# Own PSUM tiles for weight products and transposes, and value turns one to a step, in an attention and max-out kernel

## Chip, cores and metric

One core of one Trainium2 chip runs the kernel. The metric is device time in microseconds (us), lower is better.

## The reference, cut to what matters

```python
# attention over 4 x 8 heads, sequence 768, head size 64; keys and values are first
# mixed over 8 blocks of 96 by a matrix P made from sort_net (softmax and column sums, 5 rounds)
k_sorted = einsum('bhij,bhjcd->bhicd', P, k_blocks)
v_sorted = einsum('bhij,bhjcd->bhicd', P, v_blocks)
attn = softmax(q_block @ k_sorted_block.T / 8)          # each block of 96 on its own
x = (attn @ v_sorted_block)                             # -> 3072 tokens x 512
# max-out layer
h1, h2 = x @ w1, x @ w2                                 # 512 -> 1024
return maximum(h1, h2) @ w_out                          # 1024 -> 512
```

The kernel uses max(h1, h2) = max(h1 - h2, 0) + h2. It makes g = relu(x (W1 - W2)), and for the h2 part it multiplies W2 with Wout once (the "W2 Wout product", wc), so that the output is g Wout + x wc.

## The kernel before

Batch 0 runs its attention, and the weights are prepared beside it. Later batches' attention is woven between the matmuls of the layer. Everything that TensorE (PE) writes lands in PSUM, and here in one pool of four PSUM tiles, each of two banks:

```python
psum = ctx.enter_context(tc.tile_pool(name="psum", bufs=4, space=bass.MemoryType.PSUM))
def ps_f32(name):
    return psum.tile([128, 1024], FP32, tag="ps", name=name)
def ps_bf16(name):
    return psum.tile([128, 2048], BF16, tag="ps", name=name)
```

A new tile takes a place that an earlier tile has left; its first matmul waits until the earlier tile has been evicted (copied out or read for the last time) by ScalarE (ACT, "A") or VectorE (DVE, "D"). To multiply W2 with Wout, W2 is transposed by PE in two lots of 16 blocks; the second lot is evicted half by ACT, half by DVE:

```python
    def w2_transposes(t, eng):
        ps = ps_bf16("tw_ps")
        for n in range(16):
            fb, dmt = t * 4 + n // 4, n % 4
            nc.tensor.matmul(
                ps[:, n * 128 : (n + 1) * 128],
                w2_sb[:, dmt, fb * 128 : (fb + 1) * 128],
                ident,
                is_transpose=True,
                start=True,
                stop=True,
            )
        def out():
            w = 2048 // len(eng)
            for n, e in enumerate(eng):
                evac(
                    w2T[:, t * 4 : t * 4 + 4, :].rearrange("p f d -> p (f d)")[
                        :, n * w : (n + 1) * w
                    ],
                    ps[:, n * w : (n + 1) * w],
                    w,
                    two_x=True,
                    eng=e,
                )

        return out

    wc_ps = {}

    def w_product(dmt, eng=None):
        m = dmt % 2
        if m == 0:
            wc_ps[0] = ps_f32("wc_ps")
        for fb in range(NFB):
            nc.tensor.matmul(
                wc_ps[0][:, m * 512 : (m + 1) * 512],
                w2T[:, fb, dmt * 128 : (dmt + 1) * 128],
                wo_sb[:, fb, :],
                start=(fb == 0),
                stop=(fb == NFB - 1),
            )
        if m == 1:
            evac(wc[:, dmt - 1 : dmt + 1, :].rearrange("p t n -> p (t n)"), wc_ps[0], 1024, eng=eng)
```

So two products share one tile, which is held from the first product to the end of the second. The order of the steps that the change touches (cut; the comments are added here):

```python
tail = {
    ...
    3: [
        VA[6],                                  # values 6: attention output, step 6 of steps 0 to 7
        VA[7],
        lambda: w2_transposes(1, "AD")(),
        lambda: x_transposes(0, 2, "A"),
        lambda: [turn(second, c) for c in (0, 12, 24)],
    ],
    ...
# batch 0, weaving in batch 1's attention: value turns (a DVE copy that reorders values for batch 2)
VA[1:6] = [(lambda f=f, g=g: (f(), g())) for f, g in zip(VA[1:6], tns)]
TR[0:2] = [(lambda f=f, g=g: (f(), g())) for f, g in zip(TR[0:2], tns[5:])]
SC[7:] = [lambda f=SC[7], g=tns[7]: (f(), g())]
```

`TR[0]` runs in the same step as `VA[1]`, so two turns stand in a row behind values 1. A values step ends with a reciprocal and a multiply (x) on DVE, which free its PSUM tile.

The softmax here doesn't subtract the row's maximum and nothing guards it: scores larger than these inputs give would overflow.

## Time and profile before

| | before |
|---|---|
| median of 3 runs | 171.54 us (171.15 to 171.66) |
| span of the profiled run | 169.6 us |
| PE busy | 162.3 us, 96% |
| DVE, ACT busy | 54%, 47% |
| share of PE in the chain that ended last | 87% |

A line of the timeline has the start, the length, engine and source line, the operation, output <- inputs with shapes, how many instructions were merged, and in brackets the idle time before it and what ended that. A line of the chain has start, length, and engine, tile and source line. The chain is found from the last instruction backwards: at each step what released it, or the instruction before it on its engine. A matmul's end is modelled by the profiler; its start is recorded. PEld is PE's weight load. The tiles in these lines: o_ps is the attention output of a values step, s_ps the scores, tq_ps query transposes, tx_ps x transposes, v_ps the mixing ("sort") of the values, tw_ps and w2T the transposed W2, wc_ps the W2 Wout products, h_ps and out_ps the layer's two matmuls.

### The profile page before, as it was taken

How to read it: one execution, taken by the hardware profiler on the slowest of the kernel's cores; microseconds unless marked ns; L12 is line 12 of the kernel's file. 1: busy time of each engine (PE TensorE's matmuls, PEld its weight loads, DVE VectorE, ACT ScalarE, POOL GpSimd, SP SyncE). 2: the span in 40 equal slices, each digit the busy share in tenths (PEclk: the TensorE clock that was granted, in tenths of full speed). 3: DMA queues.
4: the chain of work that ended last, by engine and by line, in shares of the span. 5: the costliest groups of instructions: out<-in, count | busy, mean ns of one | idle time of the engine just before them, and what ended most of it. 6: DMA issues, size and time to landing. Idle time of an engine off the chain costs nothing.

```text
span 169.6 us, 4551 instructions
## 1 busy us (share of the span) xinstructions
PE 162.3 (96%) x2015; PEld 97.0 (57%) x2015; DVE 91.8 (54%) x198; ACT 80.4 (47%) x98; POOL 25.3 (15%) x40
## 2 busy tenths in 40 slices
PE   7799999999999999999999999999999999999991
PEld 7638766736666554457665545566554546654461
DVE  4979677689245399847674448074552422330040
ACT  3598975756855554046774350446505404312000
POOL 7944372243300000000510000000000000000000
PEclk9999999999999999999999999999999999999999
DMA  3999999999999652994199349930025173000342
GB/s 47 201 206 207 199 207 206 209 202 206 215 220 198 106 170 52 140 238 151 10 199 169 92 126 215 194 120 6 0 50 150 34 203 128 0 0 0 124 157 94
DMA packets 29811, 23.11 MB, mean 136 GB/s; under 512 B 16672, under 2 KB 24736, under 8 KB 29792
## 3 DMA queue, kind: packets, MB, share of 16 engines
q0 software_dynamic: 10304, 12.58, 43.7%
q1 hardware_dynamic: 19200, 10.04, 23.9%
q8 instruction: 16, 0.26, 0.6%
q10 hardware_dynamic: 288, 0.20, 0.4%
q14 instruction: 3, 0.02, 0.0%
HBM read 25.17 MB, written 6.29 MB: 186 GB/s over the span
## 4 chain that ended last, share of the span: by engine, by line
PE 87%; DVE 6%; ACT 3%; DMA 1%; issue 1%
PE out_ps L608 37%; PE h_ps L581 26%; PE o_ps L471 5%; PE k_ps L377 4%; PE s_ps L444 4%; PE wc_ps L559 3%; PE v_ps L398 2%; PE v_ps L419 1%; PE tw_ps L529 1%; PE tq_ps L347 1%; DMA p_sb<-in_sort_net_dram 1%; PE tq_ps L352 1%; DVE colsum L226 1%; PE o_ps L81 1%; PE tx_ps L509 1%
## 5 line engine op out<-in xcount | busy, mean ns | idle before, releaser
L608 PE MATMUL out_ps<-wo_sb,g 128*128 128x512 bf16 (+2 forms) x208 | 48.3, 363 | 0.0
L581 PE MATMUL h_ps<-xT,w_sb 128*128 128x384 bf16 x256 | 44.8, 326 | 0.2 <-ACT g L595 0.2
L581 PEld LDWEIGHTS <-w_sb 128*128 128x128 bf16 x256 | 24.0, 98 | 15.7 <-issue 0.2
L452 ACT ACTIVATE e<-s_ps 96x768 bf16<-96x768 f32 x32 | 24.2, 804 | 16.1 <-PE s_ps L444 15.9
L608 PEld LDWEIGHTS <-g 128*128 128x128 bf16 x208 | 17.5, 97 | 15.3
L595 ACT ACTIVATE g<-h_ps 128x768 bf16<-128x768 f32 x21 | 16.9, 810 | 18.0 <-PE h_ps L581 18.0
L608 PE MATMUL out_ps<-wc,xT 128*128 128x512 bf16 (+2 forms) x104 | 25.0, 362 | 0.0
L103 ACT COPY o<-out_ps 128x1024 f32<-128x1024 f32 x9 | 9.1, 1012 | 30.0 <-PE out_ps L608 25.7
L597 DVE TENSOR_SCALAR g<-h_ps 128x768 bf16<-128x768 f32 x11 | 10.5, 955 | 22.5 <-PE h_ps L581 22.5
L488 DVE TENSOR_TENSOR x<-o_ps,rs 96x512 bf16<-96x512 f32 x32 | 22.0, 687 | 1.1
L482 DVE RECIPROCAL rs<-o_ps 96x8 f32<-96x8 f32 x32 | 6.4, 199 | 20.5 <-PE o_ps L471 20.4
L608 PEld LDWEIGHTS <-xT 128*128 128x128 bf16 x104 | 9.9, 97 | 11.0
L209 DVE COPY v_dc<-v_raw 64x768 bf16<-64x768 bf16 (+2 forms) x18 | 15.4, 897 | 0.1
L471 PEld LDWEIGHTS <-e 96*128 96x128 bf16 x256 | 11.6, 97 | 6.7 <-DVE x L488 0.5
L471 PE MATMUL o_ps<-v_sb,e 96*128 96x65 bf16 x256 | 12.9, 193 | 0.1
L105 DVE CAST v_sb<-v_ps 96x1024 bf16<-96x1024 f32 x7 | 8.5, 1214 | 5.6 <-PE v_ps L398 5.2
L103 ACT CAST v_sb<-v_ps 96x1024 bf16<-96x1024 f32 x9 | 8.9, 1014 | 1.6 <-PE v_ps L419 1.0
L444 PEld LDWEIGHTS <-kT 64*128 64x128 bf16 x256 | 6.0, 94 | 5.4 <-issue 4.6
L444 PE MATMUL s_ps<-qT,kT 64*128 64x96 bf16 x256 | 8.6, 204 | 0.1
L103 ACT CAST kT<-k_ps 128x1024 bf16<-128x1024 f32 x8 | 7.7, 1021 | 1.1 <-PE k_ps L377 1.1
L105 DVE COPY o<-out_ps 128x1024 f32<-128x1024 f32 x2 | 2.4, 1224 | 10.6 <-PE out_ps L608 9.5
L81 PEld LDWEIGHTS <-fill 128*128 128x128 bf16 x109 | 6.9, 120 | 2.2 <-DVE fill L72 1.2
(76 smaller groups left out, 138.4 us busy)
## 6 DMA issues: line engine op xcount, KB each, us to landing
out_dram<-o SPq DMA_DIRECT2D x11, 512.0 KB, 3.1
k_raw<-in_k_dram POOLq DMA_DIRECT2D x12, 256.0 KB, 10.3
q_raw<-in_q_dram POOLq DMA_DIRECT2D x4, 768.0 KB, 12.6
v_raw<-in_v_dram POOLq DMA_DIRECT2D x6, 384.0 KB, 13.8
w_sb<-in_moe_w_dram POOLq DMA_DIRECT2D x3, 512.0 KB, 15.9
wo_sb<-in_moe_w_out_dram POOLq DMA_DIRECT2D x2, 512.0 KB, 18.8
v_raw<-in_v_dram POOLq DMA_DIRECT2D x3, 256.0 KB, 4.9
w_sb<-in_moe_w_dram POOLq DMA_DIRECT2D x2, 256.0 KB, 14.1
```

The costliest lines, as they stand in the source:

```text
L81: nc.tensor.matmul(ps[:, 0:w], w0, fill[:, 0:w], start=True, stop=True)
L103: nc.scalar.copy(out=out_ap, in_=in_ap)
L105: nc.vector.tensor_copy(out=out_ap, in_=in_ap)
L209: nc.vector.tensor_copy(out=dst, in_=src)
L444: nc.tensor.matmul(ps[:, h2 * 512 + ii * 128 : h2 * 512 + ii * 128 + BLK], kT[b][rows, (hp * 8 + i) * BLK : (hp * 8 + i) * BLK + 128], rhs ...
L452: nc.scalar.activation(out=e[:, 0 : 8 * BLK].rearrange("p (t c r) -> p t c r", t=8, r=R), in_=ps[0:BLK].rearrange("p (t f) -> p t f", t=8) ...
L471: nc.tensor.matmul(ps[:, h2 * 512 + ii * 65 : h2 * 512 + (ii + 1) * 65], e[:, (h2 * 4 + ii) * BLK : (h2 * 4 + ii) * BLK + 128], v_sb[:, m0 ...
L488: nc.vector.tensor_tensor(out=x, in0=ov[:, :, :, 0:D], in1=rs.to_broadcast([BLK, 2, 4, D]), op=ALU.mult,)
L581: nc.tensor.matmul(h_ps[t][:, m * 512 : m * 512 + TCH], w1_sb[:, hp, fb * 128 : (fb + 1) * 128], xT[:, b % 2, ch, hp % 2, hp // 2, :], sta ...
L595: nc.scalar.activation(out=g, in_=src, func=AF.Relu)
L597: nc.vector.tensor_scalar(out=g, in0=src, scalar1=0.0, scalar2=None, op0=ALU.max)
L608: nc.tensor.matmul(dst, g_tiles[b, ch, m // 2][:, m % 2, off : off + 128] if m < NFB else xT[:, b % 2, ch, hp % 2, hp // 2, off : off + 12 ...
```

## The change

The intent: no tile of products is held over other work, each half of the second transposes is in its own tile so that neither evicting engine waits for the other, the transposes come one step sooner so that their eviction lies beside the last values, and none of the eight turns for batch 2 stands directly behind another on DVE.

```diff
--- before.py
+++ after.py
@@ -523,48 +523,47 @@
     wc = big.tile([128, HP, DMODEL], BF16, tag="wc", name="wc")
 
     def w2_transposes(t, eng):
-        ps = ps_bf16("tw_ps")
-        for n in range(16):
-            fb, dmt = t * 4 + n // 4, n % 4
-            nc.tensor.matmul(
-                ps[:, n * 128 : (n + 1) * 128],
-                w2_sb[:, dmt, fb * 128 : (fb + 1) * 128],
-                ident,
-                is_transpose=True,
-                start=True,
-                stop=True,
-            )
+
+        w = 16 // len(eng)
+        outs = []
+        for p, e in enumerate(eng):
+            ps = ps_bf16("tw_ps")
+            for n in range(w):
+                fb, dmt = t * 4 + (p * w + n) // 4, n % 4
+                nc.tensor.matmul(
+                    ps[:, n * 128 : (n + 1) * 128],
+                    w2_sb[:, dmt, fb * 128 : (fb + 1) * 128],
+                    ident,
+                    is_transpose=True,
+                    start=True,
+                    stop=True,
+                )
+            outs.append((ps, p, e))
+
         def out():
-            w = 2048 // len(eng)
-            for n, e in enumerate(eng):
+            for ps, p, e in outs:
+                fb = t * 4 + p * w // 4
                 evac(
-                    w2T[:, t * 4 : t * 4 + 4, :].rearrange("p f d -> p (f d)")[
-                        :, n * w : (n + 1) * w
-                    ],
-                    ps[:, n * w : (n + 1) * w],
-                    w,
+                    w2T[:, fb : fb + w // 4, :].rearrange("p f d -> p (f d)"),
+                    ps[:, 0 : w * 128],
+                    w * 128,
                     two_x=True,
                     eng=e,
                 )
 
         return out
 
-    wc_ps = {}
-
     def w_product(dmt, eng=None):
-        m = dmt % 2
-        if m == 0:
-            wc_ps[0] = ps_f32("wc_ps")
+        ps = ps_f32("wc_ps")
         for fb in range(NFB):
             nc.tensor.matmul(
-                wc_ps[0][:, m * 512 : (m + 1) * 512],
+                ps[:, 0:512],
                 w2T[:, fb, dmt * 128 : (dmt + 1) * 128],
                 wo_sb[:, fb, :],
                 start=(fb == 0),
                 stop=(fb == NFB - 1),
             )
-        if m == 1:
-            evac(wc[:, dmt - 1 : dmt + 1, :].rearrange("p t n -> p (t n)"), wc_ps[0], 1024, eng=eng)
+        evac(wc[:, dmt, :], ps[:, 0:512], 512, eng=eng)
 
 
     g_tiles = {}
@@ -719,8 +718,8 @@
         2: [SC[6], SC[7], VA[5]],
         3: [
             VA[6],
+            lambda: w2_transposes(1, "AD")(),
             VA[7],
-            lambda: w2_transposes(1, "AD")(),
             lambda: x_transposes(0, 2, "A"),
             lambda: [turn(second, c) for c in (0, 12, 24)],
         ],
@@ -789,9 +788,8 @@
                 tail[9][2:2] = ks
                 vs = [lambda t=t: sort_v(1, t) for t in range(4)]
                 tns = [lambda c=c: turn(both, c) for c in range(0, BLK, 12)]
-                VA[1:6] = [(lambda f=f, g=g: (f(), g())) for f, g in zip(VA[1:6], tns)]
-                TR[0:2] = [(lambda f=f, g=g: (f(), g())) for f, g in zip(TR[0:2], tns[5:])]
-                SC[7:] = [lambda f=SC[7], g=tns[7]: (f(), g())]
+                for step, n in [((VA, 0), 0), ((VA, 1), 1), ((VA, 2), 2), ((VA, 4), 3), ((TR, 1), 4), ((VA, 5), 5), ((SC, 7), 6), ((VA, 6), 7)]:
+                    step[0][step[1]] = lambda f=step[0][step[1]], g=tns[n]: (f(), g())
                 steps = group(*vs[:3]) + qs[:1] + group(*SC[0:2], vs[3]) + qs[1:] + VA[:1]
                 steps += group(*SC[2:5]) + VA[1:2]
             elif b == 1:
```

## The prediction

> **What bounds the kernel now.** I read the page first: the busy shares, then the chain of work that ended last.
>
> ```profile
> PE 162.3 (96%) x2015; PEld 97.0 (57%) x2015; DVE 91.8 (54%) x198; ACT 80.4 (47%) x98; POOL 25.3 (15%) x40
> ...
> PE 87%; DVE 6%; ACT 3%; DMA 1%; issue 1%
> ```
>
> TensorE (PE) is busy 96% of a 169.6 us span and has 87% of the chain; VectorE (DVE) and ScalarE (ACT) are half idle. The clock row of the page is nine tenths or more in all 40 slices. So a change that only gives DVE or ACT less to do moves nothing. It has to remove time in which PE streams nothing. Where is such time in the part that the change touches? The chain of waits between 30 and 54 us, in order of time (start, length, what), shows each place where the chain leaves PE:
>
> ```profile
> 32.69 0.91 PE tw_ps L529 x16
> 33.60 0.02 issue
> 33.62 1.02 ACT w2T L103
> 34.64 0.02 issue
> 34.66 0.70 DVE w2T L105
> 35.37 0.05 issue
> 35.41 0.60 PE wc_ps L559 x2
> ...
> 47.60 1.02 ACT v_sb L103
> 48.62 0.04 issue
> 48.66 0.83 PE tq_ps L347 x12
> ...
> 51.25 1.02 ACT wc L103
> 52.27 0.04 issue
> 52.32 0.83 PE tq_ps L347 x12
> ```
>
> There are three. First, the W2 Wout product waits for the two halves of the second W2 transposes, evicted by ACT and then by DVE. Second, a query transpose waits for a value eviction. Third, the next query transpose waits for the eviction of the wc pair. From 53.15 us to 114 us the chain has PE pieces alone.
>
> A length on the chain is not a loss: PE works beside most of it. What PE loses is read from the waits view of this stretch:
>
> ```profile
> DVE w2T L105 <- ACT w2T L103: 0.4, 1, 0.4
> PEld L559 <- ACT w2T L103: 0.4, 1, 0.4
> ...
> PE tq_ps L347 <- ACT wc L103: 0.2, 1, 0.2
> ...
> PE tq_ps L347 <- ACT v_sb L103: 0.2, 1, 0.2
> ```
>
> The timeline gives the last two as 0.19 and 0.16 us. The weight loads of L559 waited 0.39 us (for ACT) and 0.61 us (for DVE), but loads run ahead of matmuls, so PE lost less. The timeline says how much:
>
> ```profile
> 33.76 2.26 PE L559 MATMUL wc_ps<-wo_sb,w2T 128*128 128x512 bf16 x8
> ...
> 35.85 0.51 PE L509 MATMUL tx_ps<-ident,x 96*128 96x96 bf16 x8
> ```
>
> Eight products of 512 columns took from 33.76 to 35.85, 2.09 us from start to start. Six products of that shape without waits take 1.30 us in the chain (out_ps x6), 0.217 each, so eight need 1.73. PE lost 2.09 - 1.73 = 0.36 us here. With the other two, **0.36 + 0.16 + 0.19 = 0.71 us** is all that this stretch has to give: 0.4% of the span.
>
> **What the Trainium skill says.** "TensorE: Matmul & The Clock Gate", section "Back-to-back issue gap", gives N/2.4 + 2.5 ns for a warm matmul of N columns, 216 ns for 512; the 0.217 us above agrees, so a product in a stream is already at that pace and only gaps can go. "Trace Analysis", section "Matmuls", says independent matmul groups should rotate through different PSUM banks so that the eviction of one overlaps the next. That is the intent here; the trace agrees, with DVE's half of w2T starting only when ACT's half had ended (the 0.4 us above). "ScalarE: Activation LUTs", section "What ACT_TABLE_LOAD costs", says back-to-back ACTIVATEs overlap by about 93 ns. The trace agrees: the w2T copy started at 33.62 and took 1.01, and the next ACT copy started at 34.53, 0.10 before its end. I use this below.
>
> **The change, part by part.** A comparison of the instruction orders shows the same number of PE instructions (4032 rows) and of DVE copies, with the same engine for each eviction; two evictions of wc on ACT become four. Matmul work is the same. The pool has four PSUM tiles taken in turn, so each tile waits for the eviction of the tile four takes earlier, and I follow that.
>
> *1. Second W2 transposes in two tiles, before the last values.* Before, values 6 and 7 start at 32.04 (16 matmuls, 0.49 us to the next start), then 16 transposes start at 32.53. After, values 6 end their slots at 32.04 + 0.245 = 32.285, and the transposes start there. A slot is (1.06 - 0.22)/15 = 0.056 us, so the first eight end at 32.285 + 7 x 0.056 + 0.22 = 32.90, the second eight at 33.35. ACT is in the relu of h_ps (32.24 for 0.81) until 33.05, and can start its half 0.10 us earlier than that end, at 32.95; at 1.01 us it ends at 33.96. DVE has value 6's multiply until 33.41, then its half (0.69) until about 34.07. It no longer waits for ACT: the comparison of orders shows its wait as one on PE now.
> The catch: the first product of W2 Wout takes the tile that ACT just evicts. In the order, its first matmul now has the wait on ACT that the fifth had before. So four products that used to run beside ACT's copy now wait. PE is ready at 33.76 and starts at 33.96 + 0.05 = 34.01. It then runs without a gap (DVE's part is needed only at 34.01 + 6 x 0.217 = 35.31) and ends its slots at 34.01 + 1.73 = 35.74, against 35.85. **Gain 0.11 us of the 0.36**; the other 0.25 becomes a wait at the front. Value 7's multiply moves to about 34.2 to 34.9 on DVE; the transposes that need it come at 35.74, so it stays hidden.
>
> *2. Products in own tiles.* A pair tile is held over the value sorts and the first query transpose, which leaves three tiles to turn. That is why the query transpose waited for the first value eviction until 48.62. After, it takes the tile of product 2, whose matmuls end near 46.95. ACT's key evictions end at 47.11; then a 512-wide copy. From 372 ns for 256 and 1012 ns for 1024 columns, 0.83 ns a column, I estimate 0.585 us, so the tile is free at about 47.7, well before PE comes at 48.50. **Gain 0.16 us.** ACT does the two value evictions 0.5 us later; nothing waits for them until the score products at 51 us. The second query transpose takes product 3's tile: matmuls end at 51.23, plus 0.585 instead of 1.01 gives about 51.85, and PE comes at 52.32 - 0.19 = 52.13. **Gain 0.19 us.** The cost is two more ACT copies, 4 x 0.585 against 2 x 1.012, 0.3 us of an engine that idles over half the time: nothing on the path.
>
> *3. Value turns, one to a step.* Eight copies of 0.82 us on DVE stay eight, spread out from one step earlier. Between 54 and 72 us the windows view has PE busy 18.00 of 18.00 us (DVE 14.24): no wait for DVE is there to remove. **Gain 0.** The first turn now comes at about 55.7 and needs value loads that landed by 39.24 + 14.0 = 53.2 us; the fifth needs those landing at 42.56 + 12.5 = 55.1. They do not stall it.
>
> Sum: 0.11 + 0.16 + 0.19 = 0.46 us, all before 54 us. Downstream PE is the bound, so it passes to the end whole: 169.6 - 0.46 = 169.1 us of span, and 171.54 - 0.46 = **171.1 us**.
>
> **The rivals.**
> (a) *The new front wait eats part 1.* If ACT cannot start its half until the relu has fully ended (33.05 instead of 32.95), or the first product is released later, part 1's 0.11 goes to zero or slightly below, and the time is about 171.2. For it: the order shows that wait, and the margin is a tenth. Against: the overlap seen on ACT.
> (b) *The whole 0.71 us is recovered.* That needs ACT's half to land by 33.7, 0.25 us earlier than its relu allows. It would make 170.8.
> (c) *The turns hurt or help.* A turn ahead of a value multiply could hold a PSUM tile 0.8 us longer, so that PE waits between 55 and 72 us. For it: DVE is busy 1.97 of each 2 us from 60 to 66. Against: spreading avoids the back-to-back pairs of 1.56 us that stand there now, without any wait of PE. Loss or gain up to 0.3 us.
> (d) *The end is set by something else,* the loads say. Against: the chain has only 1% DMA, and PE never waits after 54 us in the touched part.
>
> **Range and chances.** Gains of 0.2 to 0.8 us cover (a) to (c). The three runs before span 171.15 to 171.66, so the noise of a median, some 0.25 us, is as large as the effect. I take 170.6 to 171.6. Two per cent would be 3.4 us, five times all the PE idle time in reach, so faster by over 2% has 1%; slower by over 2% would need a new stall of 3 us, also 1%.
>
> **What would show it.** Right: the weight loads of L559 wait no more for DVE's w2T; the first product starts near 34.0 and the next transposes near 35.74 (0.1 earlier); both waits of tq_ps are gone; pieces after 53 us start 0.4 to 0.5 us earlier; PE stays gapless to 72 us; span about 169.1. Wrong: the first product starts at 33.76 (then (b)), o_ps or s_ps gain waits on DVE (then (c)), or the gain at 53 us shrinks again before the end, which would mean that another wait takes over downstream.

## The result

| | before | after |
|---|---|---|
| first measurement, median of 6 runs | 171.41 us | 170.84 us |
| ratio | | 0.9962 (95% interval 0.9939 to 0.9986) |
| measured again later | 171.53 us (11 runs) | 170.65 us (6 runs), ratio 0.9958 (0.9938 to 0.9977) |
| span of the profiled run | 169.6 us | 169.2 us; 168.8 when taken again |

A ratio is the mean time of one kernel's fast runs over that of the other's in the same rounds, so it is not quite the ratio of the medians. One of the twelve runs of the changed kernel took 693 us at full clock; it counts as slow and is in no ratio, it did not come again in the six later runs, and what caused it is open. It is counted in the median of 170.84 us; the five runs beside it have a median of 170.62 us.

The chain of waits of the changed kernel, around the second transposes:

```profile
32.42 0.89 PE tw_ps L533 x16
33.31 0.24 PE o_ps L471 x8
33.56 0.40 PE tx_ps L509 x8
33.96 0.02 issue
33.98 1.89 PE wc_ps L559 x8
```

The chain as printed does not leave PE here any more. The first product starts at 33.98, later than before (33.76), and then runs its eight matmuls without a gap. But one wait for w2T is still there, and the chain does not show it. The timeline after:

```profile
32.92 1.01 ACT L103 COPY w2T<-tw_ps 128x1024 bf16<-128x1024 bf16 x1
...
33.44 0.51 PE L509 MATMUL tx_ps<-ident,x 96*128 96x96 bf16 x8
...
33.98 1.89 PE L559 MATMUL wc_ps<-wo_sb,w2T 128*128 128x512 bf16 x8
...
35.70 0.51 PE L509 MATMUL tx_ps<-ident,x 96*128 96x96 bf16 x8
```

From the eight x transposes to the product it is 0.54 us (33.44 to 33.98), and was 0.34 before (33.42 to 33.76). The product starts 0.05 us after ACT's copy ends (33.93), and in the build its first matmul waits for that copy. The 0.20 us are hidden because the modelled end of the transposes is 33.95. Without gaps the eight products take 1.72 us from start to start (33.98 to 35.70), against 2.09 before.

Next, the two places where a query transpose waited. The timeline of PE, before:

```profile
46.93 1.57 PE L398 MATMUL v_ps<-bd,v_dc 64*128 64x64 bf16 x48
48.66 0.83 PE L347 MATMUL tq_ps<-ident,q_pair 128*128 128x128 bf16 x12 [0.16 <-ACT v_sb L103]
...
51.50 0.63 PE L398 MATMUL v_ps<-bd,v_dc 64*128 64x64 bf16 x16
52.32 0.83 PE L347 MATMUL tq_ps<-ident,q_pair 128*128 128x128 bf16 x12 [0.19 <-ACT wc L103]
```

and after:

```profile
46.77 1.57 PE L398 MATMUL v_ps<-bd,v_dc 64*128 64x64 bf16 x48
48.28 0.84 PE L347 MATMUL tq_ps<-ident,q_pair 128*128 128x128 bf16 x12
...
51.13 0.63 PE L398 MATMUL v_ps<-bd,v_dc 64*128 64x64 bf16 x16
51.69 0.84 PE L347 MATMUL tq_ps<-ident,q_pair 128*128 128x128 bf16 x12
```

Both waits are gone. Look at the starts: from the value sorts to the transposes took 1.73 us and takes 1.51, a difference of 0.22, where the bracket says 0.16. The second pair went from 0.82 to 0.56, a difference of 0.26, where the bracket says 0.19. **The bracket is too small by 0.06 to 0.07 us both times.** That is how far the modelled end lies past the pace without a wait: after the change the transposes start at 48.28, 0.06 before the modelled end of the sorts (46.77 + 1.57 = 48.34), and at 51.69, 0.07 before it (51.13 + 0.63 = 51.76).

Last, the stretch with the value turns, where the prediction expected nothing. The timeline before:

```profile
59.16 1.56 DVE L209 COPY v_dc<-v_raw 128x768 bf16<-128x768 bf16 x2
...
60.88 0.69 DVE L488 TENSOR_TENSOR x<-o_ps,rs 96x512 bf16<-96x512 f32 x1
...
61.29 0.67 PE L444 MATMUL s_ps<-qT,kT 64*128 64x96 bf16 x16
...
61.90 0.61 PE L608 MATMUL out_ps<-wo_sb,g 128*128 128x512 bf16 x2
```

and after:

```profile
58.51 0.83 DVE L209 COPY v_dc<-v_raw 128x768 bf16<-128x768 bf16 x1
...
59.50 0.69 DVE L488 TENSOR_TENSOR x<-o_ps,rs 96x512 bf16<-96x512 f32 x1
...
60.65 0.51 PE L444 MATMUL s_ps<-qT,kT 64*128 64x96 bf16 x16
...
61.09 0.61 PE L607 MATMUL out_ps<-wo_sb,g 128*128 128x512 bf16 x2
```

Sixteen score matmuls, two tiles of eight, took 0.61 us from start to the next start (61.29 to 61.90) and take 0.44. No idle time is printed before. But DVE's multiply of values 2 ended at 60.88 + 0.69 = 61.57, in the middle of the sixteen, because two turns in a row (1.56 us) had stood before it. In the build of the kernel before, the second score tile has the PSUM banks of the values 2 tile: its matmuls had to wait for that multiply. The timeline merges the sixteen; asked with `--window 61.64:61.95`, it starts the second eight at 61.62, and after the change, with `--window 60.99:61.15`, at 60.83. So the second eight started 0.33 us after the first before (61.29 to 61.62), 0.05 after the multiply's end, and 0.18 us after it now (60.65 to 60.83). The difference is the 0.15 us that b_turns measures.

### The profile page after: what moved, and what is told of

The parts are those of the page before. It is cut to its first block, busy times and chain, and to the rows that moved or that the text cites. A ratio compares the mean times of both kernels' runs of the same rounds, so it can differ in the third digit from the quotient of the medians.

```text
span 169.2 us, 4551 instructions
## 1 busy us (share of the span) xinstructions
PE 162.1 (96%) x2015; PEld 97.4 (58%) x2015; DVE 92.1 (54%) x198; ACT 80.6 (48%) x100; POOL 24.7 (15%) x40
## 4 chain that ended last, share of the span: by engine, by line
PE 87%; DVE 8%; issue 1%; ACT 1%; DMA 1%
PE out_ps L607 37%; PE h_ps L580 24%; PE o_ps L471 5%; PE wc_ps L559 4%; PE k_ps L377 4%; PE s_ps L444 3%; PE v_ps L398 2%; PE v_ps L419 1%; PE tw_ps L533 1%; DMA p_sb<-in_sort_net_dram 1%; PE tx_ps L509 1%; PE tq_ps L352 1%; PE tq_ps L347 1%; DVE x L488 1%; DVE colsum L226 1%
```

## The experiments

All traces are compared by the starts of PE's matmuls, cut into stretches. Values 6 is where the touched part begins (31.97 to 32.11 us in all runs).

| run | 1: values 6 to last x transposes | 2: to first output product | 3: to first h product of batch 1 | to the last matmul | last matmul to end of span |
|---|---|---|---|---|---|
| before | 3.82 | 17.17 | 19.80 | 92.99 | 3.76 |
| after | 3.69 | 16.67 | 19.65 | 92.99 | 4.22 |
| after, again | 3.69 | 16.67 | 19.65 | 92.99 | 3.78 |
| a_products | 3.82 | **16.67** | 19.82 | 92.99 | 3.55 |
| b_turns | 3.82 | 17.17 | **19.65** | 92.99 | 3.46 |
| c_transposes | **3.69** | 17.17 | 19.80 | 92.99 | 3.60 |
| d_two_tiles | **3.92** | 17.17 | 19.80 | 92.99 | 3.85 |
| e_turn_dose | 3.69 | 16.67 | **20.54** | 92.99 | 4.09 |
| f_product_first | 1 and 2 together **20.12** | | 19.65 | 92.99 | 3.72 |

The fourth column is the same to the hundredth in all: what is won before 73 us is passed on whole. The last column, the last matmuls and the final store, scatters between 3.46 and 4.22 us whatever the kernel; that is why the first pair of profiles differs by 0.34 us in span where the last matmul starts 0.80 us sooner.

| run | median | runs over those of before | 95% interval |
|---|---|---|---|
| a_products | 170.90 us | 0.9969 | 0.9947 to 0.9992 |
| b_turns | 171.30 us | 0.9992 | 0.9973 to 1.0011 |
| c_transposes | 171.36 us | 0.9994 | 0.9972 to 1.0016 |
| d_two_tiles | 171.68 us | 1.0016 | 0.9996 to 1.0035 |
| e_turn_dose | 171.66 us | 1.0013 | 0.9992 to 1.0034 |
| f_product_first | 170.53 us | 0.9944 | 0.9926 to 0.9963 |
| after, again | 170.65 us | 0.9958 | 0.9938 to 0.9977 |

The kernel before had a median of 171.44 us in the rounds of the first four and 171.53 us in those of the last three. All gave correct results. By time alone b, c, d and e can't be told from the kernel before; the trace tells them apart.

### a_products: own tiles for the products alone

```diff
-        m = dmt % 2
-        if m == 0:
-            wc_ps[0] = ps_f32("wc_ps")
+        ps = ps_f32("wc_ps")
...
-        if m == 1:
-            evac(wc[:, dmt - 1 : dmt + 1, :].rearrange("p t n -> p (t n)"), wc_ps[0], 1024, eng=eng)
+        evac(wc[:, dmt, :], ps[:, 0:512], 512, eng=eng)
```

> The kernel before, with own PSUM tiles for the four W2 Wout products and nothing else of the change. Stretches are read from start to start on TensorE: stretch 1 from values 6 to the second x transposes (3.81 us before, 3.69 after), stretch 2 from there to the first output product (17.17 before, 16.67 after), stretch 3 from there to the first h product of the next batch (19.81 before, 19.65 after). The prediction's theory (the idle time that the profile prints, 0.16 + 0.19 us): stretch 2 loses 0.35 us, to 16.82. Rival (printed idle time starts at the modelled end of a matmul, so each wait is 0.07 us larger than printed): stretch 2 loses 0.48 to 0.50 us, to about 16.68, and the whole gain of stretch 2 belongs to this part. Stretches 1 and 3 as before under both. Time 0.2 to 0.3% less than before.

Measured: stretch 2 is 16.67 us, 0.50 less, the whole of what the changed kernel wins there, and 1 and 3 stay. The rival holds: the waits were 0.22 and 0.26 us and not 0.16 and 0.19 (the 0.02 us left are rounding and the transposes behind the waits). The edit does two things, own tiles and evictions of 512 in place of 1024 columns (0.58 us in place of 1.01), and the runs don't part them.

### b_turns: the turns alone

```diff
-VA[1:6] = [(lambda f=f, g=g: (f(), g())) for f, g in zip(VA[1:6], tns)]
-TR[0:2] = ...
-SC[7:] = ...
+for step, n in [((VA, 0), 0), ((VA, 1), 1), ((VA, 2), 2), ((VA, 4), 3), ((TR, 1), 4), ((VA, 5), 5), ((SC, 7), 6), ((VA, 6), 7)]:
+    step[0][step[1]] = lambda f=step[0][step[1]], g=tns[n]: (f(), g())
```

> The kernel before, with the value turns spread one to a step and nothing else. The prediction's theory: TensorE waits for nothing there, stretch 3 stays 19.81 us. Rival, from the trace after: the two turns in a row (1.56 us) before the third value multiply hold the PSUM tile of the second score product for 0.16 to 0.18 us; stretch 3 shrinks to about 19.65 us, and the 16 score matmuls near 61 us take 0.51 us in place of 0.67. Stretches 1 and 2 as before.

Measured: stretch 3 falls to 19.65 us, by 0.15, and nothing else moves. The prediction's zero for this part was wrong.

### c_transposes: two transpose tiles, one step sooner, alone

```diff
 (w2_transposes as in the change)
         3: [
             VA[6],
+            lambda: w2_transposes(1, "AD")(),
             VA[7],
-            lambda: w2_transposes(1, "AD")(),
```

> The kernel before, with the second W2 transposes in two PSUM tiles and before the last values; products still in pairs, turns as before. Theory: the first product waits for the ACT half and starts 0.2 us later than before against values 6, then runs without a gap; stretch 1 is 3.69 to 3.70 us (0.11 to 0.12 less than before). Rival (the gain of stretch 1 needs own tiles of the products as well): 3.81. Stretches 2 and 3 as before.

Measured: stretch 1 is 3.69 us, 0.13 less, as in the changed kernel. The three parts add up: 0.50 + 0.15 + 0.13 = 0.78 us, and the changed kernel's three stretches together are 0.78 us shorter (40.79 to 40.01).

### d_two_tiles: two transpose tiles, not sooner

The edit of c_transposes without its second part: the step list stays as before.

> The kernel before, with the second W2 transposes in two PSUM tiles but left after the last values. Theory (each tile waits for the eviction four tiles earlier): the first product now takes the tile of values 7, whose multiply on DVE ends at about 34.25, so it starts near 34.3 instead of 33.76, and stretch 1 grows by 0.15 to 0.2 us, to about 4.0. Rival (two tiles alone free DVE from waiting for ACT and are the gain): stretch 1 shrinks to 3.7 or less.

Measured: the first product starts at 34.27 and stretch 1 is 3.92 us, 0.10 longer than before. So two tiles alone are a loss in the trace, and the step sooner is what turns the part into a gain. But the reason given in the expectation does not hold. The build gives the first product the banks of the first transpose tile, as in the changed kernel, and not those of values 7; its first matmul has a wait on ACT and none on values 7's multiply. ACT's half of w2T ran from 33.20 to 34.21 here and from 32.92 to 33.93 in the changed kernel: 0.28 us later, and the product starts 0.29 us later (34.27 against 33.98). The timeline of this run:

```profile
33.20 1.01 ACT L103 COPY w2T<-tw_ps 128x1024 bf16<-128x1024 bf16 x1
...
33.59 0.69 DVE L488 TENSOR_TENSOR x<-o_ps,rs 96x512 bf16<-96x512 f32 x1
...
34.27 1.89 PE L563 MATMUL wc_ps<-wo_sb,w2T 128*128 128x512 bf16 x7 [0.19 <-ACT w2T L103]
```

The product starts at 34.27, before the multiply's end (33.59 + 0.69 = 34.28). That the multiply would have ended near the same time was chance. And "four tiles earlier" is only mostly how the pool hands out places. (One of the eight matmuls is missing from this trace.)

### e_turn_dose: three turns in a row

```diff
-[((VA, 0), 0), ((VA, 1), 1), ((VA, 2), 2), ...
+[((VA, 1), 0), ((VA, 1), 1), ((VA, 1), 2), ...
```

> The changed kernel, but with the first three value turns in a row behind values 1 (the kernel before had two in a row there, the changed one has one). Theory (the turns in a row delay the third value multiply, and with it the PSUM tile of the second score product near 61 us): with one in a row TensorE waits 0 us there, with two 0.18 us, with three about 0.18 + one turn of 0.77 = 0.95 us; stretch 3 grows from 19.65 to about 20.6 us. Rival (stretch 3 shrank in the changed kernel because the first turn comes one step earlier, not because turns in a row hold a tile): stretch 3 is 19.8 us as in the kernel before. Stretches 1 and 2 as after.

Measured: stretch 3 is 20.54 us, 0.89 more than in the changed kernel. With one, two and three turns in a row it is 19.65, 19.80 and 20.54; the third turn adds 0.74, one turn's slot. Here the wait is long enough to be printed (timeline of this run):

```profile
58.48 2.29 DVE L209 COPY v_dc<-v_raw 128x768 bf16<-128x768 bf16 x3
...
60.61 0.34 PE L444 MATMUL s_ps<-qT,kT 64*128 64x96 bf16 x8
...
60.93 0.69 DVE L488 TENSOR_TENSOR x<-o_ps,rs 96x512 bf16<-96x512 f32 x1
...
61.67 0.34 PE L444 MATMUL s_ps<-qT,kT 64*128 64x96 bf16 x8 [0.72 <-DVE x L488]
```

The second eight start when the multiply has ended (60.93 + 0.69 = 61.62). This is the mechanism of the kernel before, magnified. Of the 0.89 us that were lost the bracket shows 0.72: again it is short.

### f_product_first: a version past the changed one

The wait that is left in stretch 1 is that of the first product for its tile, until ACT has evicted its half. In this version the product comes before values 7, where its tile is that of the h product, free since the relu:

```diff
         3: [
             VA[6],
             lambda: w2_transposes(1, "AD")(),
+            lambda: w_product(0, "A"),
             VA[7],
...
-        4: [lambda: x_transposes(0, 3, "A"), load_rest, ...
+        4: [load_rest, ...
...
-            units += wps[:2]
+            units += [lambda: None, lambda: w_product(1, "A", lambda: x_transposes(0, 3, "A"))]   # run after its fourth matmul
```

> The changed kernel, but with the first W2 Wout product straight behind the second W2 transposes, ahead of values 7 and their x transposes (the last x transposes go into the middle of the second product). Four tiles earlier is then the h tile, which the relu frees at 33.05 us, so the product has its tile without the wait of 0.19 us that is left in the changed kernel, and its first four matmuls run beside ACT's half of the eviction. Theory: from values 6 to the first output product 20.36 us shrink by 0.19 to about 20.17. Rival (the wait moves to value 7's multiply, which comes 1.4 us later: the last x transposes or the first h products wait for it): 20.36 or more. Time 0.1% below the changed kernel, within the noise of it; the trace decides.

> The changed kernel as it is, beside the run above and against the kernel before. Theory: from values 6 to the first output product 20.36 us, stretch 3 19.65 us, time 0.3 to 0.45% below before; the run of 693 us seen once does not come again if it was not the kernel's doing.

Measured, f_product_first: 20.12 us from values 6 to the first output product, 0.24 less than the changed kernel's 20.36: about 0.20 of the product's wait and 0.05 before it, where the changed kernel's x transposes start at 33.44, 0.05 after DVE's multiply of values 6 (32.70 + 0.69 = 33.39), and come 0.29 us after values 7, here 0.24. The time is 170.53 us against 170.65 in the same rounds, in the direction of the trace but inside the noise. The timeline of this run:

```profile
32.92 1.01 ACT L103 COPY w2T<-tw_ps 128x1024 bf16<-128x1024 bf16 x1
...
33.15 1.89 PE L559 MATMUL wc_ps<-wo_sb,w2T 128*128 128x512 bf16 x8
...
36.33 0.51 PE L509 MATMUL tx_ps<-ident,x 96*128 96x96 bf16 x8
```

The product starts at 33.15, beside ACT's copy, not after it. By the trace it is the shortest of the versions run; by time it can't be told from the changed kernel. The changed kernel, run again beside it, came as expected: 20.36 and 19.65 us, 0.42% below the kernel before, and no run of 693 us.

## Why the prediction was right

The time lay within the range of 170.6 to 171.6 us, but close to its lower end: 171.1 was predicted, 170.84 measured first (170.62 without the 693 us run) and 170.65 later. By its steps:

- **PE's gaps are all there is to win:** right. Each part's gain is a PE gap, and later stretches pass it on unchanged (92.99 us in all runs).
- **Transposes, 0.11 us:** right, 0.13 measured (3.82 to 3.69, in c_transposes alone too). The front wait came as worked out: ACT's copy started at 32.92, 0.10 before the relu's end (32.21 + 0.81 = 33.02), the first product at 33.98 (34.01 predicted) and the next transposes at 35.70 (35.74).
- **Products, 0.16 + 0.19 = 0.35 us:** the mechanism was right (the 512-wide copy took 0.58 us, 0.585 estimated), the size not: 0.50 us (a_products). The step that failed is the reading "The timeline gives the last two as 0.19 and 0.16 us". Those brackets count from the modelled end of the last matmul, and without a wait the next one starts 0.06 to 0.07 us before that end. From start to start the same waits are 0.26 and 0.22.
- **Turns, "Gain 0":** wrong, 0.15 us (b_turns). The step that failed is "PE busy 18.00 of 18.00 us (DVE 14.24): no wait for DVE is there to remove". A score matmul's span is 0.20 us long in the trace while eight of them start within 0.15 us, so a hole of 0.15 us is covered by the span of the matmul before it. It is the same error as in the point above, in a view that sums spans. Rival (c) allowed a loss or a gain of up to 0.3 us here, for a turn put ahead of a multiply; what it took to be "without any wait of PE", the pair of turns that stands there before, was the wait.
- **Sum:** 0.46 predicted, 0.78 in the trace, 0.65 to 0.72 us by the ratios (0.38% and 0.42% of 171.4). The miss of 0.3 us stayed inside the range because that was made wide enough for the noise of runs and for gains up to 0.8 us. That 170.8, the time given for rival (b), came close to the measured one is luck: (b) did not happen, and what was won beyond the sum came from the products and the turns.
- **Signs:** the waits, the first product, the next transposes and the unbroken PE to 72 us came as listed. The sign "pieces after 53 us start 0.4 to 0.5 us earlier" failed: the first output product starts 0.65 us earlier (53.02 to 52.37), the first h product of batch 1 0.80 (72.83 to 72.02). And "PE stays gapless" could not tell right from wrong, since the view had no gap before either, with a hole of 0.15 us in it.
- **Rivals:** (a) and (b) did not happen in the changed kernel; what (b) asked for, the rest of the 0.36 us, is what f_product_first gets, by another tile rather than a faster ACT.
- **Four tiles in turn:** right for the places that the prediction followed in the changed kernel, wrong as a rule (d_two_tiles).
- **PSUM banks:** the 0.4 us by which DVE's half waited for ACT's is a wait between two evictions of one tile. It is no sign of what the prediction cites beside it, matmuls that overlap the eviction of another tile; a_products is (0.50 us).

The Trainium skill's page "Perfetto Trace Analysis", section "Identifying the Most-Contended Engine", (the prediction calls the page "Trace Analysis") says that matmul busy share is no good measure of how close a kernel is to its roofline, because pipelined instructions look smaller in the trace, and its section "Tensor Engine Instruction (MATMUL, LD_WEIGHTS)" that their end is estimated. The trace agrees that the share misleads, to the point that a stretch of 100% hid a hole of 0.15 us. But the reason here is the other way round: the score matmuls look longer than their slots, 0.20 us each where eight start within 0.15 us.

## What to carry to other kernels

On an engine whose ends are modelled, measure a wait from start to start against the same group without the wait, never from the printed idle time or busy share alone. When a tile holds several results, ask what else must turn in the tiles that are left; give a result its own tile where it would be held over other work. On the engine that frees PSUM tiles, put long copies that nobody waits for one at a time between the short ones that others wait for.

## What the Trainium skill lacked or had wrong

- "Perfetto Trace Analysis", section "Tensor Engine Instruction (MATMUL, LD_WEIGHTS)": it says that the end is a model, but not what follows for gaps. Idle times of PE that count from that end are too small: 0.16 printed for 0.22 us, 0.19 for 0.26, 0.72 for 0.89, and nothing for 0.15.
- "TensorE: Matmul & The Clock Gate", section "Back-to-back issue gap": it gives some 131 ns a matmul for N = 512 in real streams of weight load and matmul, and 81 ns for N = 128, as what is sustained. Here such streams run at the isolated gap that it gives beside them: 0.217 us for 512 columns, 0.056 us for the 128-column transposes.
- "Perfetto Trace Analysis", section "Matmuls": it says to rotate groups through PSUM banks, but not that which eviction a group waits for depends on the order of the steps. The same two transpose tiles were worth -0.13 us one step sooner and +0.10 us in the old place.
